# Pacing of attention under the middle pair of batches, and when the last pair's x operands are made

## The chip, the cores and the metric

The kernel runs on one core of a Trainium2 chip. The metric is the device time of one execution in microseconds (us); lower is better. Engines go by the profile's names: PE is TensorE's matmul, PEld its weight load, DVE is VectorE, ACT is ScalarE, POOL is GpSimd, and SP is SyncE, whose one queue issues all the kernel's transfers.

## The reference

Block-local attention with a block summary, followed by a mixture of four experts, each a two-layer network:

```python
# attention: B, H, S, D = 4, 8, 768, 64; block 32, window 16
k_sum = k.reshape(B, H, nb, block, D).max(axis=3)
v_sum = v.reshape(B, H, nb, block, D).mean(axis=3)
scores_l = where(|i - j| < window, scale * q @ k.T, -1e9)
scores_s = scale * q @ k_sum.T + log(block)
a = softmax(concatenate([scores_l, scores_s]))
x = a @ concatenate([v, v_sum])          # -> (3072 tokens, 512)
# experts: E = 4, F = 1024
p = domain_probs / domain_probs.sum(-1)
for e in range(E):
    h = maximum(x @ w1[e], 0)
    out += p[:, e:e+1] * (h @ w2[e])
```

## The kernel before

**Pieces of attention.** Attention is cut into 64 pieces, numbered n: a batch, one of eight blocks of 96 queries, and one of two groups of four heads. A piece goes through steps that are written as a list, sorted by a key: `load_piece` (keys `kr`, queries and values `qv`), `stage_a` (splits them in high and low parts: `ks`, `qs`, `v`), `scores` in two halves (matmuls into `psc`, DVE maxima `ms` and `nb`, ACT exponentials), `probs` (weights `aw`), `transposed` (a transposing transfer to `awT`), `values` (matmuls into `px`), and `to_x`. The last step of piece n has the key n + 1.12 + 2.3, so the last of all, of piece 63, has 66.42. In `to_x`, for batches 1 to 3, the result `xs` is stored to a tile `xd` in DRAM, one tile for a quarter (96 queries) of a pair of half batches.

**Experts.** Tokens are in 8 half batches of 384. The first two are done by plain matmuls; the others by pairs, pair 1, 2 and 3 (batches 1, 2 and 3). For a pair, the first layer multiplies 2 by 2 blocks with seven products instead of eight (`SEVEN`, with banks a, d, b, c: `pha`, `phd`, `phb`, `phc`; six matmuls a product and group). Within one such block of seven groups m = 0 to 6, ACT copies bank a to bank b after m = 0 (`phb<-pha`) and bank d to a temporary after m = 1 (`p<-phd`); m = 2 adds to bank b, DVE makes bank c of it (`phc`), m = 4 adds to b and DVE adds it to bank d (`phd`). ACT and DVE turn the banks into `h`. The second layer (`po`) is plain for pairs 1 and 2 and by sevens for pair 3 (`poa` to `pod`). While the first layer of one expert runs, the second layer of the expert before it is mixed in; the second layer of a pair's last expert stands alone at the end of the pair.

**x operands.** The first layer of a pair needs seven sums and differences of the pair's x blocks, each as a high and a low float16 part. `x_operands` takes seven tiles and returns four parts, one for each quarter: a part loads `xr` from `xd` and issues 7 casts on ACT, 7 differences on DVE and 4 on POOL. For pair 3, whose second layer is by sevens too, `w2_operands` makes such sums of the second weights (`wr`, scaled and split to `w2g`) in sets; four sets of the first expert are issued in the last second layer of pair 2 (`fetch7`).

**What sets the order.** The main loop runs over a plan of six stages: two half batches alone, both together, then pairs 1, 2 and 3. It takes units of matmul work, and before each it issues all steps of attention whose key lies below a line: from the stage's start to its end in the table `ENDS`, in proportion to the work done (the first expert's first layer of a pair counts 0.6). The parts of the next pair's x operands are issued in the same loop, one after a unit, when the quarter's four stores have been issued. Tiles are allocated and instructions reordered by the scheduler of the language, which keeps priorities by the place in this program and simulates when an instruction could start; within an engine the order is then fixed.

```python
                advance(pos + (end - pos) * min(1.0, done / paced))

                if nxt < NTB // 2 and u > whole - second_us + 1e-3:
                    if parts is None:
                        xpair[nxt], parts = x_operands(nxt)
                    if parts and written.get((nxt, TB // QB - len(parts))) == 4:
                        parts.pop(0)()
```

Here `u` is the work done in the stage, `whole` all of it and `second_us` one second layer, so that the condition holds in the last expert's second layer alone. Nearly all instructions of the profile have line 75, that of a helper, and are told apart by the names of their tiles.

Of the kernel before, what the change touches and what calls it, by code (L numbers as in the profile page):

```python
# [27 lines left out]
NTB = B * S // TB  # L28
# [4 lines left out]
NEG = -1.0e9 / SCALE  # L33

SHIFT = 1.12
ENDS = (17.52, 25.5, 38.0, 53.0, 68.0, 70.0)
WARM = 11

KEYS = (1.38, 3.85, 1.13, 11.28, 5.91, 6.72, 13.44, 18.09, 21.41, 52.74, 24.82, 23.32, 21.81, 24.25, 59.33, 71.64, 6.83, 9.12)
# [23 lines left out]
def attn_moe(ctx: ExitStack, tc: tile.TileContext, qvL, qv0, v0L, kD, kT, vT, w1L, w2L, dpL, cst, out):  # L63
# [134 lines left out]
    written = {}  # L198
# [254 lines left out]
    def x_operands(pr):  # L453
        both = {w: sb.tile([P, 2, 2, TB], F16, name=f"x{pr}_{w}", tag="x", bufs=NX) for w in XS}
        xp = {w: (x[:, 0], x[:, 1]) for w, x in both.items()}

        def split(w, raw, c, lo):
            hi, low = (x[:, :, c : c + QB] for x in xp[w])
            A.copy(hi, raw)
            lo.tensor_tensor(low, raw, hi, op=ALU.subtract)  # L460

        def part(ib):
            raw = sb.tile([P, 4, 2, QB], F32, name=f"xr{pr}_{ib}", tag="chunk", bufs=CHUNKS)
            SP.dma_start(raw, xraw.pop((pr, ib)))
            b11, b12, b21, b22 = (raw[:, k] for k in range(4))
            c = ib * QB
            split("11", b11, c, PL)
            V.tensor_tensor(b11, b12, b11, op=ALU.subtract)
            split("22", b22, c, PL)
            V.tensor_tensor(b12, b22, b12, op=ALU.subtract)  # L470
            V.tensor_tensor(b22, b22, b11, op=ALU.subtract)
            split("t2", b22, c, V)
            split("t1", b11, c, PL)
            split("t3", b12, c, V)
            split("21", b21, c, PL)
            V.tensor_tensor(b21, b21, b22, op=ALU.subtract)
            split("t4", b21, c, V)

        return xp, [lambda ib=ib: part(ib) for ib in range(TB // QB)]
# [280 lines left out]
    def issue_deferred(all_of_them=False):  # L760
        for d in deferred:
            d[0] -= 1
        while deferred and (all_of_them or deferred[0][0] <= 0):
            _, issue, a = deferred.pop(0)
            issue(*a)
# [161 lines left out]
    SEVENS = (3,)  # L927
# [65 lines left out]
    def plain_units(tbs, e, early=0, last=False):  # L993

        hT = {}
        w1, w2 = kept.pop(e, ({}, {}))
        kept.clear()
        order = [*w1, *(fc for fc in range(FC) if fc not in w1)]
        held = {}

        def mm1(fc, tb, w, c0=0, c1=KC):
            if c0 == 0:
                held[fc, tb] = ps_mm.tile([P, 512], F32, name=f"ph{tb}_{e}_{fc}", tag="mm")[:, :TB]
            ph = held[fc, tb]
            whi, wlo = (x.rearrange("p (c f) -> p c f", f=P) for x in w)
            for c in range(c0, c1):
                xh, xl = (x[:, c % 2, :] for x in xT[tb][c // 2])
                PE.matmul(ph, whi[:, c, :], xh, start=c == 0, stop=False)
                PE.matmul(ph, whi[:, c, :], xl, start=False, stop=False)
                PE.matmul(ph, wlo[:, c, :], xh, start=False, stop=c == KC - 1)  # L1010
            if c1 == KC:
                to_h(hT, tb, e, fc, ph)
            return 3 * US1 * (c1 - c0), 1.0

        for fc in range(early):
            w1[fc] = weights(w1L, e, fc, "1", PL)
            yield mm1(fc, tbs[0], w1[fc], 0, KC // 2)
        for fc in order:
            if fc not in w1:
                w1[fc] = weights(w1L, e, fc, "1", PL)  # L1020
            for tb in tbs:
                yield mm1(fc, tb, w1[fc], KC // 2 if fc < early else 0)
            if fc not in w2:
                w2[fc] = weights(w2L, e, fc, "2", V if len(tbs) == 1 else PL)
            if 1 in tbs:
                largest(e, fc, 0, w1[fc][0])
                largest(e, fc, 1, w2[fc][0])
        kept[e] = {fc: w1[fc] for fc in order[-4:]}, w2
        if 1 in tbs:
            scales_of_weights(e)  # L1030
        units = second(tbs, e, hT, w2, False)
        yield from with_fetch(units) if last else units
# [9 lines left out]
    def pair_units(pr, es, last=False):  # L1042


        tbs = (2 * pr, 2 * pr + 1)
        if pr in SEVENS:
            for e in es:
                hs = {}
                kept.clear()
                for us in first(pr, tbs, e, hs, None, None):  # L1050
                    yield us, 1.0
                yield from second_sevens(pr, tbs, e, hs)
            return
        behind = None
        for n, e in enumerate(es):
            hT = {}
            w2 = kept.pop(e)[1] if pr > 1 and e in kept else ready2.setdefault((pr, e), {})
            kept.clear()
            units = first(pr, tbs, e, hT, w2, "hl"[n % 2])
            if behind is None:  # L1060
                for us in units:
                    yield us, SLOW
            else:
                todo_us = 0.0
                for us in units:
                    yield us, 1.0
                    todo_us += us * second_share
                    while todo_us > 0.0:
                        us2, _ = next(behind, (todo_us, 0))
                        todo_us -= us2  # L1070
                        if _:
                            yield us2, 1.0
                yield from behind
            if n < len(es) - 1:
                behind = tile_by_tile(tbs, e, hT, w2)
        kept[e] = {}, w2
        yield from with_fetch(second(tbs, e, hT, w2, last), early7=(0, 3, 6, 9) if pr + 1 in SEVENS else ())
# [183 lines left out]
    def advance(to):  # L1261
        nonlocal at
        while at < len(steps) and steps[at][0] < to:
            steps[at][1](steps[at][2])
            at += 1
# [14 lines left out]
    pos = per  # L1280
    for (tbs, experts), end in zip(plan, ENDS):
        pair = tbs if isinstance(tbs, int) else None
        n = 2 if pair else len(tbs)
        first_us, second_us = n * FC * 3 * KC * US1, n * (TB // P) * FC * 3 * US2
        first_us *= 7 / 8 if pair else 1
        whole = len(experts) * (first_us + second_us)
        paced = len(experts) * (first_us + second_us) - (first_us * (1.0 - SLOW) if pair else 0.0)
        nxt = pair + 1 if pair else 1 if n == 2 else NTB
        parts, u, done = None, 0.0, 0.0
        for e in experts[:1] if pair else experts:  # L1290
            if pair:
                units = pair_units(pair, experts, last=nxt == NTB // 2)
            else:
                units, ahead = ahead or plain_units(tbs, e, last=n == 2 and e == experts[-1]), None
            for us, pace in units:
                issue_deferred()
                u += us
                done += us * pace
                advance(pos + (end - pos) * min(1.0, done / paced))

                if nxt < NTB // 2 and u > whole - second_us + 1e-3:
                    if parts is None:
                        xpair[nxt], parts = x_operands(nxt)
                    if parts and written.get((nxt, TB // QB - len(parts))) == 4:
                        parts.pop(0)()
        issue_deferred(True)
        advance(end)
        for part in parts or ():
            part()
        pos = end  # L1310
# [61 lines left out]
```

## Time and profile before

| | |
|---|---|
| median of 3 runs | 1174.93 us (1173.01 to 1178.81) |
| the profiled execution | 1173.76 us |
| its span, first to last instruction | 1172.0 us |
| mean granted clock of TensorE | 0.978 |
| instructions | 20540 |
| moved by DMA | 184.11 MB, 157 GB/s on average |

The profile is of one execution. Its first part has each engine's busy time, its second the span in 40 slices of 29.3 us, with the busy share in tenths and the clock that TensorE was granted. A row of the timeline has the start in us, the length in us, the engine, the line, the instruction with its output and inputs, how many such instructions follow each other, and in brackets how long the engine stood idle before it and what ended that.

### The profile page before, as it was taken

Reading aid. Unit: us, or ns where it says so; the run is one execution under the profiler, and the core shown is the slowest. Engines: PE = TensorE matmul, PEld = TensorE weight load, DVE = VectorE, ACT = ScalarE, POOL = GpSimd, SP = SyncE. Lnnn points to the kernel's source line nnn. Section 1 sums busy time; section 2 is a strip of 40 time slices with the busy share of each in tenths; the row PEclk is TensorE's granted clock in tenths of the full one; section 3 lists DMA queues with packets and bytes.
Section 4 is the critical chain, followed back from the end, with each engine's and each line's share of the span. In section 5 each row is a group of like instructions: output and inputs, shape, how many; then the busy total and the mean of one; then the engine's idle time right before and its main releaser. Section 6 shows DMA issues by size and latency. Waiting matters only on the chain.

```text
span 1172.0 us, 20540 instructions
## 1 busy us (share of the span) xinstructions
PE 1101.6 (94%) x6994; PEld 757.0 (65%) x6994; DVE 816.7 (70%) x1959; ACT 694.1 (59%) x1882; POOL 549.3 (47%) x650
## 2 busy tenths in 40 slices
PE   9899698999999889889979999999999989999998
PEld 7888587898897545445545455555555448686867
DVE  6888879875888667676887554544554778787784
ACT  5767466664557787877665344444442556566661
POOL 2588456772736767786653221221210434344340
PEclk9999888999999899999989999999999989999999
DMA  6476656663845767876784544364631242323201
GB/s 241 142 224 172 183 150 183 167 171 93 246 117 150 220 215 252 266 233 226 222 297 128 176 130 138 121 174 139 196 89 39 74 153 76 128 90 127 69 15 55
DMA packets 169306, 184.11 MB, mean 157 GB/s; under 512 B 79344, under 2 KB 115184, under 8 KB 169200
## 3 DMA queue, kind: packets, MB, share of 16 engines
q1 hardware_dynamic: 169200, 182.79, 51.4%
q8 instruction: 55, 0.90, 0.3%
q14 instruction: 51, 0.42, 0.1%
HBM read 131.76 MB, written 34.08 MB: 142 GB/s over the span
## 4 chain that ended last, share of the span: by engine, by line
PE 34%; DVE 9%; DMA 3%; ACT 3%; issue 2%; POOL 1%; SPq 0%; POOLq 0%; DVEq 0%; ACTq 0%
PE po L75 11%; PE phb L75 8%; PE pha L75 5%; PE phc L75 2%; DVE wr L75 2%; PE phd L75 2%; PE poa L75 1%; PE pob L75 1%; PE psc L75 1%; ACT wr L75 1%; DVE acc L75 1%; POOL w2g L75 1%; DVE xr L75 1%; DMA vch<-in_vT 1%; PE px L75 1%
## 5 line engine op out<-in xcount | busy, mean ns | idle before, releaser
L75 PEld LDWEIGHTS <-w1g 128*128 128x128 f16 x2016 | 195.9, 99 | 173.9 <-issue 36.4
L75 PE MATMUL po<-w2s,h 128*128 128x512 f16 x1152 | 270.8, 380 | 1.5 <-DVE h L75 1.4
L75 PEld LDWEIGHTS <-h 128*128 128x128 f16 x1584 | 152.1, 98 | 127.3 <-issue 2.5
L75 PE MATMUL phb<-x_t,w1g 128*128 128x384 f16 x864 | 166.6, 329 | 22.0 <-ACT phb L75 9.0
L75 PE MATMUL ph<-xh,w 128*128 128x384 f32 x512 | 142.7, 350 | 9.4 <-ACT xh L75 3.6
L75 POOL TENSOR_TENSOR ks<-kr,ks 128x304 fp32r<-128x304 f32 x112 | 99.0, 889 | 105.6 <-ACT ks L75 104.6
L75 PE MATMUL po<-w,hh 128*128 128x512 f32 x384 | 122.3, 397 | 0.0
L75 PE MATMUL pha<-x,w1g 128*128 128x384 f16 x576 | 115.1, 333 | 6.8 <-DVE nb L75 5.7
L75 ACT ACTIVATE ms<-ms,nb 96x152 f32<-96x152 f32 x256 | 104.2, 414 | 24.4 <-DVE nb L75 23.7
L75 POOL TENSOR_TENSOR v<-qv,v 128x256 f16<-128x256 f32 (+1 forms) x56 | 43.5, 778 | 141.0 <-ACT v L75 106.0
L75 POOL TENSOR_TENSOR w<-wr,w 128x512 fp32r<-128x512 f32 x60 | 82.4, 1381 | 53.4 <-ACT w L75 47.7
L75 PEld LDWEIGHTS ph<-xh,w 128*128 128x128 f32 x512 | 96.7, 195 | 11.7 <-ACT xh L75 4.0
L75 DVE CUSTOM_DVE_ANT_0 ms<-psc,c_sb 96x152 f32<-96x152 f32 x256 | 69.4, 305 | 38.9 <-PE psc L75 36.1
L75 PE MATMUL ph<-xl,w 128*128 128x384 f32 x256 | 88.1, 344 | 0.0
L75 PEld LDWEIGHTS po<-w,hh 128*128 128x128 f32 x384 | 71.0, 190 | 14.5
L75 POOL TENSOR_TENSOR w2g<-wr,w2g 128x256 f16<-128x256 f32 (+1 forms) x32 | 29.9, 951 | 99.6 <-ACT w2g L75 99.3
L75 PE MATMUL po<-w,hl 128*128 128x512 f32 x192 | 76.5, 399 | 0.0
L75 ACT CAST aw<-ms 96x512 f16<-96x512 f32 x112 | 49.5, 488 | 45.6 <-issue 25.5
L75 DVE TENSOR_TENSOR aw<-ms,aw 96x512 f16<-96x512 f32 x112 | 69.6, 654 | 7.8 <-ACT aw L75 7.6
L75 ACT CAST ks<-kr 128x304 fp32r<-128x304 f32 x112 | 48.2, 443 | 42.8 <-PE psc L75 41.9
L75 ACT CAST w<-wr 128x512 fp32r<-128x512 f32 x84 | 50.9, 616 | 31.2 <-DMA wr<-in_w1L 19.4
L75 PE MATMUL psc<-ks,qs 128*96 128x152 f32 x448 | 64.5, 271 | 4.7 <-POOL qs L75 4.6
(184 smaller groups left out, 2245.2 us busy)
## 6 DMA issues: line engine op xcount, KB each, us to landing
wr<-in_w2L SPq DMA_DIRECT2D x104, 256.0 KB, 3.2
wr<-in_w1L SPq DMA_DIRECT2D x76, 256.0 KB, 3.2
qv<-in_qvL SPq DMA_DIRECT2D x56, 320.0 KB, 3.8
kr<-in_kD SPq DMA_DIRECT2D x56, 256.0 KB, 3.2
w1g<-wdg SPq DMA_DIRECT2D x28, 512.0 KB, 3.5
w1g<-wdg SPq DMA_DIRECT2D x28, 384.0 KB, 3.6
wdg<-w1g SPq DMA_DIRECT2D x16, 512.0 KB, 4.1
wd<-w2s SPq DMA_DIRECT2D x16, 512.0 KB, 4.3
```

What stands on the lines that cost most here:

```text
L75: ins = getattr(self.engine, name)(*a, **kw)
```

## The change

Two places. In the table of the stages' ends, pair 2's end goes from 68 to 72 and pair 3's from 70 to 74. Pair 2 starts at 53, so that a step of attention is issued after 15/19 of the work that it took, and the last one (66.42) at 71% of the stage's counted work, where it was 89%. And for pair 3 (the pair in `SEVENS`) the parts of the x operands are no longer tied to the last second layer of the stage ahead: each is issued after the first unit behind its quarter's last store.

```diff
-ENDS = (17.52, 25.5, 38.0, 53.0, 68.0, 70.0)
+ENDS = (17.52, 25.5, 38.0, 53.0, 72.0, 74.0)
...
-                if nxt < NTB // 2 and u > whole - second_us + 1e-3:
+                if nxt < NTB // 2 and (u > whole - second_us + 1e-3 or (nxt in SEVENS and (nxt, 0) in written)):
```

How the instructions stand changes from the end of pair 1 to the first expert of pair 3; before and after that each engine has the same order. Three places follow. In a name, the first number of `phb`, `pha`, `phd`, `p5`, `x` and `xr` is the pair; of `po`, `acc` and `h` the half batch or tile; of `ks`, `qs`, `ms`, `xs`, `px` the piece; `phb3_3_2` is bank b of pair 3, expert 3, block 2. The number at the end counts tiles.

ACT where pair 2 ends, before: the fourth set of w2 operands, then pair 3's first copies.

```order
L75 ACTIVATE wr23_6_11134<-wr23_6_11134,scalew3_4599 128x512
L75 ACTIVATE wr23_7_11136<-wr23_7_11136,scalew3_4599 128x512
L75 CAST w2g13_3_11133<-wr23_6_11134 128x256
L75 CAST w2g03_3_11132<-wr23_7_11136 128x512
L75 CAST w2g03_3_11132<-wr23_6_11134 128x512
L75 COPY phb3_3_2_11230<-pha3_3_2_11223 128x384
L75 COPY p53_3_2_11239<-phd3_3_2_11232 128x384
L75 CAST w2g13_3_11133<-wr23_7_11136 128x512
L75 COPY p53_3_3_11323<-phd3_3_3_11316 128x384
L75 COPY phb3_3_3_11314<-pha3_3_3_11307 128x384
```

ACT at the same place now:

```order
L75 CAST w2g03_2_11079<-wr23_5_11083 128x512
L75 COPY phb3_3_2_11230<-pha3_3_2_11223 128x384
L75 CAST w2g03_2_11079<-wr23_4_11081 128x512
L75 CAST w2g13_2_11080<-wr23_5_11083 128x512
L75 ACTIVATE wr23_6_11134<-wr23_6_11134,scalew3_4599 128x512
L75 ACTIVATE wr23_7_11136<-wr23_7_11136,scalew3_4599 128x512
L75 CAST w2g13_3_11133<-wr23_6_11134 128x256
L75 CAST w2g03_3_11132<-wr23_7_11136 128x512
L75 CAST w2g03_3_11132<-wr23_6_11134 128x512
L75 CAST w2g13_3_11133<-wr23_7_11136 128x512
L75 ACTIVATE r113_3_2_11255<-pha3_3_2_11223 128x384
L75 CAST h113_3_2_11257<-r113_3_2_11255 128x384
```

The copy `phb3_3_2` has moved from the fourth set into the third; PE has the groups `pha3_3_2` and `phd3_3_2` ahead of the last second layer now, and behind it begins with `phb3_3_2`.

DVE at the start of the last second layer of pair 2, before: w2 differences (`wr`) and x differences (`xr`, `x3`) of two quarters take turns.

```order
L75 TENSOR_TENSOR wr23_0_10879<-wr23_0_10879,wr23_1_10881 128x256
L75 TENSOR_TENSOR xr3_0_10904<-xr3_0_10904 128x192 x2
L75 TENSOR_TENSOR xr3_1_10950<-xr3_1_10950 128x192
L75 TENSOR_TENSOR w2g03_0_10877<-wr23_0_10879,w2g03_0_10877 128x512
L75 TENSOR_TENSOR xr3_0_10904<-xr3_0_10904 128x192
```

DVE at the first quarter now, in the middle of pair 2:

```order
L75 SCALAR_TENSOR_TENSOR h4_2_1_9856<-phb2_2_0_9667,h4_2_1_9856 128x384
L75 TENSOR_TENSOR xr3_0_9827<-xr3_0_9827 128x192 x2
L75 TENSOR_TENSOR aw0_732<-ms59_9778,aw0_732 96x512
L75 TENSOR_TENSOR aw0_732<-ms59_9778,aw0_732 96x4x24
L75 TENSOR_TENSOR xr3_0_9827<-xr3_0_9827 128x192
L75 TENSOR_TENSOR x3_t2_8542<-xr3_0_9827,x3_t2_8542 128x2x96
L75 SCALAR_TENSOR_TENSOR acc13_9134<-po4_1_1_9798,pw2_1_8887,acc13_9134 128x512
L75 TENSOR_TENSOR x3_t3_8543<-xr3_0_9827,x3_t3_8543 128x2x96
L75 TENSOR_TENSOR phc2_2_1_9926<-phb2_2_1_9894,p52_2_1_9909 128x384
```

The quarter's seven differences stand between those of attention (`aw`) and those that PE's next groups need (`phc`).

ACT at the second quarter now, also in pair 2:

```order
L75 ACTIVATE xs59_10136<-px59_10087 128x192
L75 CAST ks62_0_10188<-kr62_9957 128x2x152
L75 ACTIVATE ms61_10100,rs61_10102<-ms61_10100,nb61_10101 96x152 x2
L75 CAST x3_11_8538<-xr3_1_10149 128x2x96
L75 CAST x3_22_8540<-xr3_1_10149 128x2x96
L75 CAST x3_21_8539<-xr3_1_10149 128x2x96
L75 CAST x3_t1_8541<-xr3_1_10149 128x2x96
L75 CAST ks62_1_10191<-kr62_9957 128x2x152
L75 CAST qs62_10194<-qv62_9958 128x384
```

The casts of the quarter stand two rows behind `xs59`, whose store completes the quarter that they read; before, they stood in the last second layer.

## The prediction, made before the changed kernel was run

> **What bounds the kernel.** I read the page's busy times and slices first, then who TensorE (PE) waits for, then the timeline of the one place where it waits and that the change touches.
>
> ```profile
> PE 1101.6 (94%) x6994; PEld 757.0 (65%) x6994; DVE 816.7 (70%) x1959; ACT 694.1 (59%) x1882; POOL 549.3 (47%) x650
> PE   9899698999999889889979999999999989999998
> PEclk9999888999999899999989999999999989999999
> ```
>
> PE is busy for 94% of the span, so what can be won is idle PE, and what it costs in granted clock afterwards. A slice is 29.3 us. Slices 23 to 31 (653 to 908 us, most of the middle pair, pair 2) are full; slice 33, near 940 us, is not. Grouped by line over 653 to 908 us, the groups of PE show no idle time, as in this one (busy, mean ns, idle before):
>
> ```profile
> L75 PE MATMUL phb<-x_t,w1g 128*128 128x384 f16 x290 | 55.4, 326 | 0.0
> ```
>
> From 900 us on PE waits for this, and nothing else (total, times, longest):
>
> ```profile
> PE phb L75 <- ACT phb L75: 5.2, 1, 5.2
> PE phb L75 <- DVE phc L75: 1.5, 4, 0.6
> ```
>
> The 5.2 us are one wait, where pair 2 ends and pair 3 begins. The timeline there (start, length, engine, instruction, count, idle before):
>
> ```profile
> 908.26 31.03 PE L75 MATMUL po<-w2s,h 128*128 128x512 f16 x143
> 939.13 1.14 PE L75 MATMUL pha<-x,w1g 128*128 128x384 f16 x6
> 942.05 1.14 PE L75 MATMUL phd<-x_t,w1g 128*128 128x384 f16 x6
> 948.36 2.08 PE L75 MATMUL phb<-x_t,w1g 128*128 128x384 f16 x6 [5.17 <-ACT phb L75]
> 950.24 2.05 PE L75 MATMUL pha<-x,w1g 128*128 128x384 f16 x6
> 952.12 1.14 PE L75 MATMUL phb<-x_t,w1g 128*128 128x384 f16 x6
> ```
>
> Pair 2's last second layer (`po`, 31 us) ends at 939.1; four groups of pair 3 follow; then PE waits for ScalarE's (ACT's) copy of bank a into bank b. After the wait two groups take 1.88 us each where others take 0.98: half the clock.
>
> ACT is late because of what stands ahead of that copy in its queue:
>
> ```profile
> 910.37 1.11 ACT L75 CAST x<-xr 128x192 f16<-128x192 f32 x4
> 929.54 1.33 ACT L75 ACTIVATE wr<-wr,scalew 128x512 f32<-128x512 f32 x2
> 945.46 1.36 DVE L75 TENSOR_TENSOR wr<-wr 128x256 f32<-128x256 f32 x1 [1.65 <-POOL w2g L75]
> 947.31 0.62 ACT L75 CAST w2g<-wr 128x512 f16<-128x512 f32 x1 [2.11 <-DVE wr L75]
> 947.84 0.47 ACT L75 COPY phb<-pha 128x384 f32<-128x384 f32 x1
> ```
>
> Under the 31 us of `po`, ACT, DVE and POOL make four sets of pair 3's second weights (`wr` to `w2g`) and, mixed in, the x operands of pair 3 (`xr` to `x`). The second set's scaling begins only at 929.5; the fourth set's cast, at 947.3, stands just ahead of the copy. How much of this is x work, by the windows of `xr` alone (length, then DVE, ACT and POOL busy with counts):
>
> ```profile
> 900.00:925.00 25.00, 6.84 (x14) 3.94 (x14) 5.04 (x8) 1.00 0.18 56
> 925.00:950.00 25.00, 7.63 (x14) 4.21 (x14) 4.80 (x8) 0.90 0.27 87
> ```
>
> That is DVE 14.5 us, ACT 8.2 us, POOL 9.8 us: 28, 28 and 16 instructions, four equal quarters.
>
> **The change, part by part.**
>
> *The x operands leave the boundary (the gain).* By the new order all four quarters stand before the last `po`, and ACT's queue there holds the four w2 sets alone, with the copy `phb3_3_2` moved up to the middle of the third set. Whether it is then in time follows from what a set costs:
>
> ```profile
> 908.85 1.32 ACT L75 ACTIVATE wr<-wr,scalew 128x512 f32<-128x512 f32 x2
> 910.08 0.39 ACT L75 CAST w2g<-wr 128x256 f16<-128x256 f32 x1
> 910.61 0.67 POOL L75 TENSOR_TENSOR w2g<-wr,w2g 128x256 f16<-128x256 f32 x1 [39.64 <-ACT w2g L75]
> 911.32 0.75 DVE L75 TENSOR_TENSOR wr<-wr 128x256 f32<-128x256 f32 x1 [1.77 <-POOL w2g L75]
> 911.38 0.62 ACT L75 CAST w2g<-wr 128x512 f16<-128x512 f32 x1
> 919.44 0.41 DVE L75 TENSOR_TENSOR wr<-wr 128x256 f32<-128x256 f32 x1
> 920.85 0.68 DVE L75 TENSOR_TENSOR w2g<-wr,w2g 128x512 f16<-128x512 f32 x1
> ```
>
> One set's chain: scale 1.32, cast 0.39, POOL's difference 0.67, two DVE differences of 0.41 to 0.75, cast 0.62, DVE 0.68 and two of 0.41, cast 0.62: 5.9 to 6.6 us until ACT is free for the next. From 908.85 two sets and the first casts of a third (2.3 us) put the copy at 908.85 + 13.2 + 2.3 = 924.4, and the fourth set's end at 908.85 + 4 x 6.6 = 935.3, with three accumulations by DVE in between perhaps 937.5. PE leaves its last `po` at 939.1, or 941.1 with the two groups of pair 3 that the new order puts before it. So the copy is some 15 us early and nothing waits. What goes: from 939.13 to 952.12 PE did six groups in 12.99 us, at 0.973 each 5.84 us: **7.1 us** lost, 5.17 of it the wait and the rest the clock. What is late next there is DVE: the group after (m = 4) needs DVE's `phc`, behind the last three accumulations; they start when `po` ends and take about 0.75 each, `phc` 0.57, 3.1 us in all, and PE has four groups (3.9 us) before it. The gain lies between 0 and 7.1 + 0.4 us (a wait of 0.37 at 971.8 in pair 3's first expert may move); I take 7.1, since the copy's margin is twice the wait.
>
> *Attention in 15 of 19 parts of the time.* The table's 68 becomes 72, so a piece of attention starts every 15/19 of the former distance, with no instruction more. From 700 to 890 us the exponentials stand with
>
> ```profile
> L75 ACT ACTIVATE ms<-ms,nb 96x152 f32<-96x152 f32 x44 | 18.1, 413 | 0.7 <-DVE nb L75 0.7
> ```
>
> four a piece: 11 pieces in 190 us, 17.3 us each, 13.7 after. PE's own work is the same.
>
> *The quarters inside attention (the cost).* On the chain of waits pair 1's last `po` ends where pair 2's run of groups begins (start, length):
>
> ```profile
> 678.90 7.78 PE po L75 x36
> 686.68 0.97 PE pha L75 x6
> ```
>
> The first quarter is complete at step 60.42 of the table's 53 to 72, 39% of pair 2's work from 686.7 to 939.1: about 785 us. The others follow at two pieces' distance, over 6 x 13.7 = 82 us. What the engines carry (busy PE, PEld, DVE, ACT, POOL; clock, DMA, GB/s), in a middle stretch of pair 2, in pair 1, where the same pace stands beside weight making, and over 611 to 655 us, where pair 2's own four quarters were made beside attention:
>
> ```profile
> 775.00:800.00 25.00, 25.00 (x149) 13.44 (x148) 12.20 (x34) 11.06 (x34) 3.88 (x7) 1.00 0.64 199
> 500.00:525.00 25.00, 21.98 (x125) 11.53 (x123) 17.77 (x39) 18.95 (x50) 20.25 (x23) 1.00 0.76 246
> 611.00:655.00 44.00, 42.54 (x260) 22.39 (x260) 34.57 (x87) 25.18 (x78) 17.35 (x26) 1.00 0.55 160
> L75 PE MATMUL px<-awT,v 128*64 128x192 f16 (+1 forms) x31 | 1.9, 231 | 1.2 <-DVE h L75 1.2
> ```
>
> If all of DVE's 12.2 us grew by 19/15 it would carry 15.5 of 25, plus 14.5 x 25/82 = 4.4: 19.9; ACT 14.0 + 2.5 = 16.5. That is an upper bound, since the parts that follow PE's matmuls do not grow. The stretch from 611 to 655 has DVE at 34.57/44, 19.6 of 25, and PE lost 1.46 us there, 1.2 of it in the last row's wait. Bounds of the new loss: 0 (pair 2 now) and pair 1's rate, 3.0 of 25, from 686.7 to 908.3, 27 us, or 15 us from the first quarter on. I take the middle between 0 and the 1.46 of the nearest stretch, **0.7 us**, since DVE's true load is between those two.
>
> The quarter's own waits: its load (`xr`) reads back what the last `xs` wrote (`xd`), on SP's one queue:
>
> ```profile
> 815.50 0.33 SPq L75 DMA_DIRECT2D xd<-xs  x1
> 817.25 0.32 SPq L75 DMA_DIRECT2D xr<-xd  x1
> xr<-xd SPq DMA_DIRECT2D x2, 384.0 KB, 2.9
> 618.37 0.60 ACT L75 CAST x<-xr 128x192 f16<-128x192 f32 x2 [2.31 <-DMA xr<-xd]
> ```
>
> From the store's issue to the landing pass 1.75 + 2.9 = 4.7 us; SP stands for 1.75 of them with w1 loads and key loads behind it, as it does now for the first two quarters. ACT takes the casts in its order: in the second quarter they stand two instructions behind `xs`, so ACT may stop there for up to 3 us (2.31 in the last row), with `ks62_1`, `qs62` and an `h` behind it. PE comes to the scores that read `qs62` some 80 matmuls later, 15 us, and to the group that needs DVE's `phd` (behind that `h`) 13 us later; the quarter delays both by about 8. Covered, so nothing more is added; if that cover is gone it is 3 us a quarter, in the first rival.
>
> **Sum.** 1173.76 (the profiled execution; 1172.0 of it span) - 7.1 + 0.7 = **1167.4 us**. The profiled execution lies 1.2 below the median 1174.93, within the runs' spread of 1173.01 to 1178.81. A change of 0.5%, 5.9 us, is about what a measurement of this kernel can tell from none; the forecast, 6.4, stands just outside.
>
> **Rivals.**
>
> *Eaten up (no change).* The quarters' stalls reach PE: ACT's stop of about 3 us at two quarters, or the 1.46 at more than one of them, 3 to 6 us in all: 1173.76 - 7.1 + 4.5 = 1171.2. For it: the row of 2.31 us. Against it: that wait of ACT had no PE wait behind it, and the margins above.
>
> *The boundary stays late (no change).* If the four sets still needed until 947.9, the second block's copy, two instructions behind them, would come at 949.4, and PE, at 941.1 + 6.7 = 947.8, would wait 1.6: 1169.0. Against it: that asks for 39 us where the rows give 26.
>
> *DVE and POOL in each other's way (slower).* DVE's differences of two SBUF operands take longer while POOL works:
>
> ```profile
> 911.24 2.55 POOL L75 TENSOR_TENSOR x<-xr,x 128x192 f16<-128x192 f32 x4
> 912.68 2.55 DVE L75 TENSOR_TENSOR xr<-xr 128x192 f32<-128x192 f32 x3
> 920.04 0.34 DVE L75 TENSOR_TENSOR xr<-xr 128x192 f32<-128x192 f32 x1
> ```
>
> 0.85 each beside POOL, 0.34 alone. Moved among attention's `ks` and `qs` differences on POOL, the quarters would hold up DVE's `phc` and `phd`, for which PE waits in pair 1. If PE lost pair 1's 12% from the first quarter to the last `po` (785 to 908 us), that is 15 us: 1173.76 - 7.1 + 15 = 1181.7. It is slower by over 0.5% from a loss of 13 us on (11% of that stretch). Against it: POOL carried 20.25 of 25 in pair 1, and will carry at most 3.88 x 19/15 + 3.0 = 7.9. The Trainium skill, SBUF — State Buffer, "SBUF: two separate sides", has this as an exclusive lock: whichever of a DVE instruction with two SBUF inputs and a GpSimd instruction starts first holds the pair of ports to its end. By that rule alone, an estimate, 28 DVE instructions each behind half a POOL instruction would cost DVE, not PE, under 15 us; the rows agree with it in kind.
>
> **Chances.** First case (gain whole, loss 0 to 2): 65%, of which 50 have a loss below 1.2 and so are faster. Eaten up 17%, late boundary 8%: no change. Slower 10%. Likeliest case alone: 1165.0 to 1169.0. With the two rivals of no change, up to the whole gain lost, the range is 1165.0 (lowest run 1173.01 - 7.1 - 0.4, rounded down) to 1174.0.
>
> **What would show it.** Right: no PE wait for ACT's `phb` near the end of pair 2, `po` followed at once by `phb` at full clock, no `xr` instruction after the last `po` begins, and the last scores some 40 us earlier; pair 2's PE idle below 1.5 us. Wrong: PE waits for `phc`, `phd`, `qs` or `px` in pair 2 of over 3 us in all, or ACT still inside the w2 sets when `po` ends. Before pair 2 and behind the first blocks of pair 3 the order is the same, so both traces should agree there.

## The result, and the profile after

| | before | after |
|---|---|---|
| median of 10 runs each, us | 1177.76 (1173.01 to 1182.0) | 1169.48 (1165.54 to 1170.61) |
| the profiled execution, us | 1173.76 | 1167.77 |
| its span, us | 1172.0 | 1166.0 |

The ratio of after to before is 0.993, 95% interval 0.9914 to 0.9946: 8.2 us less, 6.4 to 10.1. (The runs of before known at the forecast were three of these ten, with a median of 1174.93.) One run of early_only, below, took 2220.89 us, far from all the others, and is left out of its median and ratio.

On the page, PE's busy share now stays at 9 from pair 2 to the last slice but one, and its granted clock is full there; before, slice 33 had an 8 in both rows.

```profile
PE 1103.9 (95%) x6994; PEld 759.3 (65%) x6994; DVE 812.5 (70%) x1959; ACT 695.1 (60%) x1882; POOL 547.3 (47%) x650
PE   8999788999999879889979999999999999999998
PEclk9999888999999899999999999999999999999999
```

Who PE waits for from 630 us to the end (total, times, longest), after. The 5.2 us for ACT's `phb` are gone, and so are 1.2 for `px` in pair 1.

```profile
PE phb L75 <- DVE phc L75: 1.5, 3, 0.5
PE phb L75 <- DVE phd L75: 0.3, 1, 0.3
```

Timeline of PE where pair 2 ends (start, length, count), after. `po` is followed by `phb` with no gap, and a group starts every 0.98 us, as at full clock (the `pha` row has two groups); there is no bracket in these rows.

```profile
912.48 31.03 PE L75 MATMUL po<-w2s,h 128*128 128x512 f16 x143
943.34 1.14 PE L75 MATMUL phb<-x_t,w1g 128*128 128x384 f16 x6
944.32 2.11 PE L75 MATMUL pha<-x,w1g 128*128 128x384 f16 x12
946.27 1.14 PE L75 MATMUL phd<-x_t,w1g 128*128 128x384 f16 x6
947.24 1.14 PE L75 MATMUL phb<-x_t,w1g 128*128 128x384 f16 x6
```

Timeline of ACT, DVE and POOL under that `po`, after: the first set's start, the first POOL and DVE steps of it, the copy, and the last set to its end.

```profile
913.06 1.32 ACT L75 ACTIVATE wr<-wr,scalew 128x512 f32<-128x512 f32 x2
914.76 1.78 POOL L75 TENSOR_TENSOR w2g<-wr,w2g 128x256 f16<-128x256 f32 x2 [33.77 <-ACT w2g L75]
915.46 1.36 DVE L75 TENSOR_TENSOR wr<-wr 128x256 f32<-128x256 f32 x1 [1.70 <-POOL w2g L75]
...
919.02 0.42 DVE L75 TENSOR_TENSOR wr<-wr 128x256 f32<-128x256 f32 x1
...
920.00 1.33 ACT L75 ACTIVATE wr<-wr,scalew 128x512 f32<-128x512 f32 x2
...
929.01 0.47 ACT L75 COPY phb<-pha 128x384 f32<-128x384 f32 x1
...
933.91 1.33 ACT L75 ACTIVATE wr<-wr,scalew 128x512 f32<-128x512 f32 x2
...
940.34 0.62 ACT L75 CAST w2g<-wr 128x512 f16<-128x512 f32 x1 [1.55 <-DVE wr L75]
940.99 0.69 DVE L75 TENSOR_TENSOR w2g<-wr,w2g 128x512 f16<-128x512 f32 x1 [0.68 <-ACT w2g L75]
942.25 2.07 DVE L75 SCALAR_TENSOR_TENSOR acc<-po,pw,acc 128x512 f32<-128x512 f32 x3 [0.56 <-PE po L75]
...
944.55 0.56 DVE L75 TENSOR_TENSOR phc<-phb,p 128x384 f32<-128x384 f32 x1
```

The sets follow each other every 6.95 us (913.06, 920.00, ... 933.91). The copy stands at 929.01, 14 us before PE needs it, and all four sets are through at 941.68, under 2 us before `po` ends.

The windows of `xr` alone, after (length, then DVE, ACT, POOL busy with counts, clock, DMA, GB/s): the four quarters lie between 799 and 900 us, inside pair 2.

```profile
775.00:800.00 25.00, 0.00 (x0) 0.60 (x2) 0.00 (x0) 1.00 0.77 231
800.00:825.00 25.00, 2.93 (x7) 1.44 (x5) 2.16 (x4) 1.00 0.53 149
825.00:850.00 25.00, 3.38 (x7) 2.14 (x7) 2.24 (x4) 1.00 0.48 128
850.00:875.00 25.00, 2.82 (x7) 2.25 (x7) 2.24 (x4) 1.00 0.44 144
875.00:900.00 25.00, 2.79 (x7) 2.27 (x7) 2.35 (x4) 1.00 0.15 50
900.00:925.00 25.00, 0.00 (x0) 0.00 (x0) 0.00 (x0) 1.00 0.11 33
```

### The profile page after: what moved, and what is told of

Same layout as the page of the kernel before. It is cut to its first block, busy times and chain, and to the rows that moved or that the text cites. A ratio compares the mean times of both kernels' runs of the same rounds, so it can differ in the third digit from the quotient of the medians.

```text
span 1166.0 us, 20542 instructions
## 1 busy us (share of the span) xinstructions
PE 1103.9 (95%) x6994; PEld 759.3 (65%) x6994; DVE 812.5 (70%) x1959; ACT 695.1 (60%) x1882; POOL 547.3 (47%) x650
```

## The experiments

The theory: the gain comes from the x operands leaving the last `po` of pair 2, and pair 2 has room for them. Rivals: it comes from the pace of attention; or pair 2 pays for the work. Ratios are to the kernel before on the same chip, with the 95% interval; before's median there was 1177.89 us for the first four rows, 1178.81 for one_early, two_early, pace51 and pace52, and 1178.48 for the rest, and a ratio need not be the quotient of two medians. The wait is PE's for ACT's copy at the start of pair 3. The edits are shown against the changed kernel.

| run | what differs from before | median, us | ratio | wait there, us |
|---|---|---|---|---|
| after_again | the whole change | 1170.03 | 0.9924 (0.9896 to 0.9952) | none |
| ends_only | the table alone | 1179.63 | 1.0002 (0.9984 to 1.002) | 4.67 + 0.98 |
| early_only | the condition alone | 1171.77 | 0.9922 (0.9895 to 0.9949) | none |
| double | the change, quarters made twice | 1171.44 | 0.993 (0.9906 to 0.9955) | none |
| one_early | the change, one quarter issued early | 1172.2 | 0.9939 (0.992 to 0.9959) | none |
| two_early | the change, two quarters issued early | 1170.3 | 0.9922 (0.9901 to 0.9944) | none |
| alloc_only | the change, tiles alone early | 1179.32 | 1.0004 (0.9983 to 1.0025) | 3.97 + 1.18 |
| early67 | the condition, pair 2's end at 67 | 1170.77 | 0.9947 (0.992 to 0.9973) | none |
| pace51 | the change, pair 1's end at 51 | 1166.9 | 0.991 (0.9888 to 0.9933) | none |
| pace51_again | the same | 1169.54 | 0.992 (0.9895 to 0.9946) | none |
| pace52 | the change, pair 1's end at 52 | 1176.7 | 0.9982 (0.9964 to 1.0) | none |
| pace51_all | pace51, pair 2's x operands early too | 1204.11 | 1.0229 (1.0205 to 1.0252) | none |

**The two halves of the change.** Ahead of them stands the change itself once more.

> The changed kernel once more, on the chip of the three others. Theory (the gain is the boundary's wait of 5.2 us and the 1.9 us at half clock behind it, less 0.7 to 0.8 us of new waits in pair 2): ratio to before 0.993 to 0.995. Rival (the gain is an accident of one profile): 0.998 to 1.002.

> Only the table is changed (72 and 74); the x operands of pair 3 stay in the last second layer of pair 2. Theory (x work leaving the boundary is the gain): ACT's copy of bank a to bank b still stands in the fourth set of w2 operands, PE still waits about 4 to 5 us for it and then runs some microseconds at half clock; ratio 0.998 to 1.002. Rival (the gain is attention being out of the way at the boundary): the wait falls below 2 us and the ratio is 0.993 to 0.996.

```diff
-                if nxt < NTB // 2 and (u > whole - second_us + 1e-3 or (nxt in SEVENS and (nxt, 0) in written)):
+                if nxt < NTB // 2 and u > whole - second_us + 1e-3:
```

> Only the condition is changed; attention keeps the old pace, so that the quarters are made at the distance of the old pace, the last one just ahead of the w2 sets. The copy then stands behind all four sets on ACT. Theory: the four sets alone take about 28 us (6.95 a set), so their end falls within 2 us of the end of the last po; PE waits 0 to 2 us and has most of the gain, ratio 0.993 to 0.996. Rival (the pace is needed: the last quarter still collides with the sets): a wait of 3 to 5 us, ratio 0.997 to 1.001.

```diff
-ENDS = (17.52, 25.5, 38.0, 53.0, 72.0, 74.0)
+ENDS = (17.52, 25.5, 38.0, 53.0, 68.0, 70.0)
```

The timeline of PE with the table alone: the wait for ACT's copy is still there, and groups take up to 2.13 us up to 961.28.

```profile
946.70 1.14 PE L75 MATMUL phd<-x_t,w1g 128*128 128x384 f16 x6
952.51 2.08 PE L75 MATMUL phb<-x_t,w1g 128*128 128x384 f16 x6 [4.67 <-ACT phb L75]
954.38 2.12 PE L75 MATMUL pha<-x,w1g 128*128 128x384 f16 x6
957.49 2.08 PE L75 MATMUL phb<-x_t,w1g 128*128 128x384 f16 x6 [0.98 <-ACT phb L75]
959.36 2.13 PE L75 MATMUL pha<-x,w1g 128*128 128x384 f16 x6
961.28 1.33 PE L75 MATMUL phb<-x_t,w1g 128*128 128x384 f16 x6
```

The timelines with the condition alone: ACT's casts of the last quarter stand where the sets begin (its very last at 918.50); its copy, though behind all four sets, is ACT's next work after 944 and waits for PE itself, and PE goes on at full clock.

```profile
913.55 0.86 ACT L75 CAST x<-xr 128x192 f16<-128x192 f32 x3 [1.44 <-DMA xr<-xd]
...
917.27 1.32 ACT L75 ACTIVATE wr<-wr,scalew 128x512 f32<-128x512 f32 x2
...
943.56 0.62 ACT L75 CAST w2g<-wr 128x512 f16<-128x512 f32 x1 [1.55 <-DVE wr L75]
948.25 0.46 ACT L75 COPY phb<-pha 128x384 f32<-128x384 f32 x1 [4.08 <-PE pha L75]
...
950.98 1.14 PE L75 MATMUL phb<-x_t,w1g 128*128 128x384 f16 x6
951.95 1.14 PE L75 MATMUL pha<-x,w1g 128*128 128x384 f16 x6
```

The change once more gave 0.9924, a little below the 0.993 to 0.995 expected of it, which its interval overlaps. So the condition brings the whole gain that can be measured here, and the table none. This is what the theory said of both, though the condition alone gained more (0.9922) than the 0.993 to 0.996 expected of it; the rival of the pace falls. With the condition alone PE's order at the boundary is as before and the copy stands behind all four sets: neither the two groups ahead of `po` nor the copy's place in the third set is needed for the gain.

**What the quarters cost pair 2.**

> The changed kernel, but each of pair 3's four quarters is loaded and made twice over (28 more casts on ACT, 28 differences on DVE and 16 on POOL, all in pair 2). Theory (pair 2 has room for this work, a quarter costs PE about 0.2 us): 0.5 to 2 us above the changed kernel, ratio to before 0.994 to 0.997. Rival (DVE and POOL get in each other's way, the slack is used up): PE waits for phc, phd, qs or px of 5 to 15 us in all, ratio 0.998 to 1.006.

```diff
         def part(ib):
+            for again in range(2 if pr in SEVENS else 1):
+                quarter(ib)
...
-            SP.dma_start(raw, xraw.pop((pr, ib)))
+            SP.dma_start(raw, xraw[pr, ib])
```

PE's waits from 690 to 1000 us with the quarters made twice are 1.3 us in all:

```profile
PE phb L75 <- DVE phc L75: 0.7, 1, 0.7
PE psc L75 <- DVE nb L75: 0.6, 1, 0.6
```

Four more quarters (28 casts, 28 + 16 differences) cost nothing that the time can tell: 0.993 beside 0.9924 for the change on the same chip. That is less than the theory's 0.994 to 0.997, and the rival that wanted 5 to 15 us falls.

**How much x work the last `po` can hold.** Two attempts to leave some quarters there:

> Paced as in the change, but only pair 3's first quarter is made early; three stay at the boundary. Theory (each quarter left among the four w2 sets holds them up by its share: 39 us from the first scaling to the last cast with four quarters, 28 with none, 2.7 a quarter): PE waits about 2.5 us (5.2 - 2.7) for ACT's copy and runs some microseconds at half clock; ratio to before 0.995 to 0.999. Rival (one late quarter, its store and load, is enough for the whole wait): 4 to 5 us of wait, 0.998 to 1.002.

> As the last one, with two quarters early and two at the boundary. Theory: the sets end 2 x 2.7 us earlier than before, PE waits 0 to 0.5 us for the copy and keeps the full clock; ratio 0.992 to 0.996. Rival (a late quarter is enough): 4 to 5 us of wait, 0.998 to 1.002.

```diff
-(nxt in SEVENS and (nxt, 0) in written)
+(nxt in SEVENS and (nxt, 0) in written and (parts is None or len(parts) > 3))
```

(For two, the 3 is a 2.) Neither theory nor rival, and that the ratio with two early lies in the theory's range is chance: no x work stood at the boundary at all. The windows of `xr` with one quarter issued early show seven casts in each window of pair 2 from 800 to 900 us:

```profile
800.00:825.00 25.00, 2.73 (x7) 2.05 (x7) 2.15 (x4) 1.00 0.48 137
825.00:850.00 25.00, 3.38 (x7) 2.14 (x7) 2.24 (x4) 1.00 0.43 105
850.00:875.00 25.00, 2.69 (x7) 2.06 (x7) 2.22 (x4) 1.00 0.61 185
875.00:900.00 25.00, 2.80 (x7) 2.26 (x7) 2.36 (x4) 1.00 0.26 78
900.00:925.00 25.00, 0.00 (x0) 0.00 (x0) 0.00 (x0) 1.00 0.01 1
```

The scheduler had pulled the other three quarters ahead of where the program issues them: their first casts stand at 834, 862 and 887 us, 34 to 86 us before the last `po` begins (920.59). So these runs say nothing of a dose, but that one early quarter is enough. What about it is enough was the next question:

> As the change, but early only the seven x tiles are made; all four quarters are issued in the last second layer as before. Theory A (in the runs with one and two early quarters the others came early because the first quarter's instructions had taken the seven tiles; the tiles' creation alone takes nothing): all x work at the boundary, a wait of 4 to 5 us for ACT's copy, ratio 0.998 to 1.002. Theory B (the creation of the tiles is what counts): x work between 800 and 900 us, no wait, 0.992 to 0.995.

```diff
-                    if parts and written.get((nxt, TB // QB - len(parts))) == 4:
+                    if u > whole - second_us + 1e-3 and parts and written.get((nxt, TB // QB - len(parts))) == 4:
```

The windows of `xr` with the tiles alone made early: the work is back at the boundary, and so are the waits (3.97 and 1.18 us) and the time. (The profile puts the first down to DVE's `acc`, which ended at 952.50; ACT's copy of the bank ended at 952.44, and PE went on at 952.50, as far behind the copy as before, 948.31 and 948.36.)

```profile
875.00:900.00 25.00, 0.00 (x0) 0.00 (x0) 0.00 (x0) 1.00 0.12 41
900.00:925.00 25.00, 3.76 (x6) 2.70 (x11) 3.46 (x6) 1.00 0.00 1
925.00:950.00 25.00, 10.77 (x22) 5.44 (x19) 6.21 (x11) 1.00 0.32 107
```

Making the tiles early takes nothing; the first quarter's own instructions must be issued early. That they take the tiles' buffers, which later tiles of the program then can't have, fits with it, but no run shows the buffers. The run also repeats, by another edit, what the table alone gave: ratio 1.0004 beside 1.0002.

A dose came from the pace instead:

> The early condition with pair 2's end at 67 instead of 72 (and pair 3's 69): attention is paced so late that three quarters are made in pair 2 and the last one only behind the four w2 sets, ACT's copy behind its casts. Theory (work on ACT and DVE ahead of the copy, past the 31 us of the last po, is what PE waits for): the sets need 28 us, the quarter's chain of casts and differences 3 to 4 more, so PE waits 2 to 6 us where pair 3 begins, some of it for x itself, and some microseconds run at half clock; ratio 0.996 to 1.001. Rival (early issue alone brings the gain, wherever the last quarter falls): 0.992 to 0.995 and a wait below 1 us.

```diff
-ENDS = (17.52, 25.5, 38.0, 53.0, 72.0, 74.0)
+ENDS = (17.52, 25.5, 38.0, 53.0, 67.0, 69.0)
```

The windows of `xr` here: the fourth quarter (7 casts) lies under the last `po`, 2.95 us of DVE and 2.26 of ACT.

```profile
900.00:925.00 25.00, 1.66 (x5) 1.02 (x3) 0.35 (x1) 1.00 0.20 60
925.00:950.00 25.00, 2.95 (x7) 2.26 (x7) 2.58 (x4) 1.00 0.47 152
```

The expectation missed: no wait of PE at the boundary. It had put the quarter end to end behind the four sets; in the trace ACT did its first casts at 935.12, in a gap that the last set leaves, and its last `w2g` cast at 935.88, before `po` ended at 939.8. The ratio and the missing wait are what the rival had said, that early issue brings the gain wherever the last quarter falls. This run can't tell the rival from another reading, that one quarter fits under the 31 us and four do not (before, 39 us from the first scaling to the cast just ahead of the copy, with one cast of the sets still to come). Two and three weren't got there by any run.

**Looking for more.** Pair 1 has idle PE, so the next question was whether attention can move from pair 1 to pair 2.

> The changed kernel with pair 1's end in the table at 51 instead of 53: attention 13/15 as fast in pair 1, 21/19 as fast in pair 2. Theory (pair 2 has room, as the quarters made twice showed at about 1 us; pair 1 loses PE to attention beside weight making, some 4 of 50 us each): 2 to 5 us faster than the changed kernel, ratio to before 0.988 to 0.991. Rival (what PE waits for in pair 1 isn't a matter of pace): as the changed kernel, 0.992 to 0.994; or pair 2's x operands come too late for pair 2's first blocks and it is slower, 0.995 to 1.000.

> As the last one with 52. Theory: half of its gain, ratio 0.990 to 0.993. Rival: as the changed kernel, 0.992 to 0.995.

> The kernel with 51 at the end of pair 1 once more. If its lead over the changed kernel is real: 0.989 to 0.992; if it was chance: 0.992 to 0.995.

```diff
-ENDS = (17.52, 25.5, 38.0, 53.0, 72.0, 74.0)
+ENDS = (17.52, 25.5, 38.0, 51.0, 72.0, 74.0)
```

51 gave 0.991 and 0.992, beside 0.993 and 0.9924 for the change: the intervals overlap, so a version better than the change isn't shown. 52 gave back most of the gain, which neither expectation had. A step of one in this table moves the time by more than the trend that was looked for. The profile of 52 has new waits after 660 us, one of 3.4 us for ACT's `h` and two of 3.0 in all for DVE's `phd`; why just there stays open. (The diff is that of 51; 52 has 52.0 in the same place.)

> The kernel with 51, and the early condition for pair 2's x operands too (made in pair 1, each as soon as its quarter is stored). Theory (the same mechanism at the boundary of pairs 1 and 2, where no w2 sets stand and the last po waited 0.7 us for h): nothing to win there, and pair 1 is the stage whose engines are full, so 0 to 5 us worse than 51 alone, ratio 0.990 to 0.996. Rival (the quarters crowd that boundary as they did the next): 1 to 4 us better, 0.987 to 0.990.

Beside the 51:

```diff
-(u > whole - second_us + 1e-3 or (nxt in SEVENS and (nxt, 0) in written))
+(u > whole - second_us + 1e-3 or (nxt, 0) in written)
```

Worse by 2.3%, far past either expectation. The windows of 350 to 450 us (PE, PEld, DVE, ACT, POOL), first this kernel, then after:

```profile
350.00:450.00 100.00, 64.28 (x379) 46.57 (x379) 71.14 (x184) 56.50 (x173) 50.20 (x68) 0.76 0.62 179
```

```profile
350.00:450.00 100.00, 85.75 (x506) 55.77 (x506) 69.98 (x183) 73.47 (x214) 66.02 (x85) 0.95 0.66 198
```

PE loses 21 us of busy time in that stretch and the clock falls to 0.76; ACT and POOL are emptier than in after, and DVE is as full, so full engines, the reason given, aren't shown as the cause. The seven x tiles come from the same 14 buffers as keys and weights of attention's odd pieces, and holding them through pair 1 would fit; that was not tried, so the cause stays open.

## Why the prediction was right

**The gain, 7.1.** Six groups of pair 3 are done when the seventh starts: 952.12 before, 947.24 after, 4.88 earlier. The last `po` starts 4.22 later (912.48, not 908.26), of which 1.95 are the two groups put ahead of it. So the boundary itself gained 4.88 + 4.22 - 1.95 = 7.15 us. With x work still there (the table alone) nothing is gained; without it (the condition alone) the gain is whole. The price of such a boundary is that of one execution, though. The time beyond 0.975 us a group, from pair 3's first group to the first at full clock again, was 7.1 us before, 9.9 with the table alone and 7.2 with the tiles alone made early; the last section has more on the clock's part in it.

**The chain of sets.** 5.9 to 6.6 us a set was too little: 6.95, since DVE's first difference takes 1.36 beside POOL, not 0.41 to 0.75 (a row of the prediction itself, at 945.46, has the 1.36). That the whole came out as forecast is luck: 28.65 us from the first scaling to the end (908.85 to 937.5), measured 28.62 (913.06 to 941.68). The forecast had short sets and some 2 us for three accumulations of DVE; in the trace these fall into gaps that DVE has anyway, and the longer sets take up the 2 us. The copy's margin, "some 15 us", was 14. DVE's `phc`, late next by the forecast, ended at 945.11, before PE's `phb` of 947.24.

**The new loss, 0.7.** PE's two waits in pair 2, after:

```profile
831.90 1.14 PE L75 MATMUL phb<-x_t,w1g 128*128 128x384 f16 x6 [0.31 <-DVE phd L75]
860.88 1.14 PE L75 MATMUL phb<-x_t,w1g 128*128 128x384 f16 x6 [0.52 <-DVE phc L75]
```

0.83 us in all. ACT stopped for the loads of the second, third and fourth quarter for 4.14, 3.57 and 4.44 us, more than the "up to 3 us" of the forecast. The cover held all the same: PE's two waits come 6 and 9 us after such a stop, and whether they stem from it is not shown, but PE waited for nothing else in pair 2. The first quarter came at 799 us, forecast 785; the last scores started at 850.51, before at 885.03, 35 us earlier and not 40.

**The pace.** It was costed at nothing, with no gain of its own: so it is, to within 0.2% (1.0002, 0.9984 to 1.002).

**The rivals.** "Eaten up" and "boundary stays late" needed waits that no row shows. For "DVE and POOL in each other's way" the mechanism is there but not its price in PE's time: the quarters' DVE time fell from 14.47 us to 11.92, which fits with fewer of them meeting POOL in pair 2, and doubling them didn't reach PE. The Trainium skill, SBUF — State Buffer, "SBUF: two separate sides", calls the port pair an exclusive lock held for a whole instruction. The trace agrees in kind: the difference that starts at 915.46, with POOL at work from 914.76 to 916.54, takes 1.36 us and ends at 916.82; the same form at 919.02 takes 0.42.

**The sum.** 1167.4 against 1167.77 for the profiled execution, from which it was made, and 1169.48 for the median. The forecast gain of 6.4 lies at the low end of the measured interval. That the two executions come out within 0.4 us of the sum is in part luck. On PE the order of the instructions differs from 711 us before (713 after) to 981 us (975 after). In that stretch after gains 7.3 us: 7.15 at the boundary and 0.58 in pair 3's first expert (0.37 of it the wait at 971.8, which the forecast had left open), less 0.39 in pair 2, where the two waits of 0.83 do not show in full. Where the order is the same, after is 1.88 later when pair 2 begins (688.40, not 686.52; a delay of 2.7 is there in the first 26 us already) and gains 0.6 at the end. No part of the change explains these two; they are differences of single executions.

## What to carry to other kernels

A wait at a boundary is bought off by moving the work that stands ahead of the late instruction to a stage where its engines have room, and both are read before the change: the length of the queue at the boundary against the cover there (39 us against 31), and the busy shares of the stage it goes to. With a reordering scheduler, where the program issues work is only a wish: one early quarter pulled the other three ahead, early tiles alone pulled none, so read the place in the trace of each variant before reading its time. The same rule one stage earlier cost 2.3%, where ACT and POOL were not fuller than before: busy shares alone don't show that there is room. And half of the change did nothing: the table alone gained nothing, and the condition alone all.

## What the runs showed of the hardware that was not expected

The half clock does not follow the length of one wait. In the kernel with 52, PE's clock drops after a wait of 1.56 us and not after one of 1.91 (timeline; a `psc` group takes 0.57 at full and 1.06 at half clock):

```profile
606.41 0.57 PE L75 MATMUL psc<-ks,qs 128*96 128x152 f32 x4 [1.91 <-POOL qs L75]
...
628.51 2.08 PE L75 MATMUL phd<-x_t,w1g 128*128 128x384 f16 x6 [1.56 <-DVE xs L75]
630.14 1.06 PE L75 MATMUL psc<-ks,qs 128*96 128x152 f32 x4
```

In each of the 14 traces the granted clock changes only at multiples of 3.41 us from its first fall. In the kernel before it fell at 945.25, 2.06 us into the wait of 5.17, and rose at 952.08. Two windows on either side of the fall, one step long each (length, then busy PE, PEld, DVE, ACT, POOL with counts; clock, DMA, GB/s):

```profile
941.84:945.25 3.41, 1.35 (x9) 0.69 (x7) 1.25 (x3) 2.73 (x5) 0.49 (x1) 1.00 0.62 180
945.25:948.66 3.41, 0.30 (x2) 0.12 (x2) 3.14 (x5) 1.35 (x3) 1.29 (x2) 0.50 0.14 50
```

With the table alone the half clock lasted from 951.42 to 961.66, three such steps with the second wait of 0.98 in them, and with the tiles alone made early from 952.54 to 955.96, one step. So the price of a wait varies with where it lies on this grid: behind the 5.17 us, 3.8 us ran at half clock, behind the 4.67 it was 8.8, and behind the 3.97 it was 3.5.

The Trainium skill, TensorE: Matmul & The Clock Gate, "What's actually happening", has the half clock come after at least one idle window of about 3.4 us that runs free of the kernel. The grid of 3.41 us agrees, and so does the 4.67: PE did nothing from 948.0 to 951.42. The 5.17 and the 1.56 do not, if idle means no matmul for a whole window: PE was busy for 1.35 us of the step ahead of the fall, and in the kernel with 52 for 1.91 (625.04 to 628.44). Busy time alone does not decide it either: in the kernel with 52 PE was busy for 1.56 us from 604.56 to 607.97, and no fall followed. What does decide it stays open.
